# An attention-and-MLP kernel: VectorE's share of the exponentials in five instructions instead of eight, with eight tile buffers and a new order of the work

## The chip, the cores and the metric

The kernel runs on one core of a Trainium2 chip. The metric is the device time of one execution in microseconds (us); the time given for a kernel is the median of its runs.

## The reference

The input x has 2048 rows of 448 numbers. Two layers follow one another, and each layer is an attention block A and a mixing block B, each on the normalised x and each added to x:

```python
x = x + _A_ref(_layernorm(x), A_wqkv, A_wo)
x = x + _B_ref(_layernorm(x), B_w1, B_w2, B_w3, B_w4)
...
scores = jnp.einsum("bhqd,bhkd->bhqk", q, k) * (Dh ** -0.5)   # 16 heads, Dh = 28
p = _softmax(scores, axis=-1)
o = jnp.einsum("bhqk,bhkd->bhqd", p, v)
...
h  = _gelu(_layernorm(x) @ w1)                  # 448 -> 448
hs = shifted_quarters(h) @ w2                   # columns moved by -1, +1, -2, +2 rows
x1 = x + hs
return x1 + _gelu(_layernorm(x1) @ w3) @ w4     # 448 -> 1792 -> 448
```

The softmax needs 2 layers x 16 heads x 2048 x 2048 exponentials.

## The kernel before

**Tiles.** The rows are 16 tiles of 128. Attention works on score blocks of 128 keys by 512 entries (512 queries of one head, or, in the last two chunks of a layer, 256 queries of one head for two key tiles). Four heads form a group g. A segment is one chunk of queries, one group and a range of key tiles; there are 68 segments, 2048 blocks in all, and they are worked off in a fixed order (`segs`, `stream`). The number of a pair of segments is the key of the tables `R_RATE` and `D_RATE`; the number of four segments is the key of `XPAR["dt", ...]` and its like.

**The way of a block.** TensorE makes the scores in PSUM (`score_ops`, L1487). ScalarE takes two or three neighbouring PSUM banks in one instruction, applies the exponential and writes bf16 tiles to the ring `PT` (`t_exp`, L1754). TensorE multiplies the tiles with the values (`t_pv`, L831) into PSUM bank 7, four heads side by side, and the last row gives the sum for the softmax's division (`t_norm`). There is no search for a maximum: a bound from the norms of q and k stands as a further row of the matrices, so each score arrives in PSUM shifted.

**Blocks for VectorE.** Some blocks go to VectorE instead of ScalarE. `d_first` (L1584) reads the scores from PSUM, multiplies them by log2(e) times 256 and stores int16 in a buffer `y`; `d_chain` (L1611 to L1624) shapes this integer in seven instructions into the bits of the bf16 exponential and writes it to a slot of `PD`: cut out the fraction (L1611), a straight line of it (L1613), its square (L1615), a straight line of the square (L1617), product (L1619), add to the integer (L1621), undo the offset and shift (L1624). There are two `y` buffers, four `PD` slots and three `fb` buffers; in two stretches of the run (`t_extra`) free parts of `vaug` give two more `y`, one more `fb` and one more `PD`. A `y` is held from before `d_first` to the end of the chain, a `PD` slot until TensorE has multiplied the block.

**Which blocks.** `t_scores` builds units of three and two blocks by turns, three PSUM banks for each. On a unit of three it may replace the third by a block from 6 to 8 steps ahead for VectorE (the ring way, `R_RATE`), if VectorE was busy in the last 3 us by less than `XPAR["dt", ...]`. It may add to any unit a block from 5 to 7 steps ahead in one of the two spare banks (the spare way, `D_RATE`), if the filler matmuls took at least the share `XPAR["ft", ...]` of the last 8 us. The two tables limit how many blocks of a segment may go each way, and each block needs a free `y` and a free `PD` slot at that moment.

**Order.** Nothing is decided on the chip. When the kernel is built, `Sched` runs the generators as tasks over modelled durations (`DST` holds those of the chain's instructions), and the order that comes out is each engine's fixed instruction list, with semaphore waits between engines. Tasks have a rank (`RANK`, smaller first); a chain's rank is `XPAR["dp", ...]` (up to 3.2) and becomes 1.0 when its block is about to be multiplied. Where TensorE would idle, `keep_pe_busy` puts in filler matmuls on `ident` (L2267), whose results nobody reads. Evictions from PSUM (L2196, L2005, L1226, L1838 and others), normalisation and additions to x run on VectorE between the chains. For a few operations `XPAR["ex", ...]` and similar entries say whether GpSimd (0), VectorE (1) or whichever is earlier (2) takes them. `PE_NORM` says for the last group of a chunk whether the softmax's division is spread with DMAs on the SP queue or with small matmuls.

## Time and profile before

| | |
|---|---|
| median of three runs | 1026.12 us (1024.83 to 1026.28) |
| profiled execution, span from first to last instruction | 1023.9 us |
| ScalarE busy / TensorE busy / VectorE busy / GpSimd busy | 973.6 / 973.4 / 843.5 / 220.1 us |
| blocks on ScalarE: units of three / of two | 332 / 459 |
| blocks on VectorE | 134 |
| granted TensorE clock | 1.000 |

The profile of the execution has a span; the time of a run is longer by what lies around it. Engines are PE (TensorE, with its weight loads as PEld), DVE (VectorE), ACT (ScalarE), POOL (GpSimd) and SP (the DMA queue). A row of the groups view gives line, engine, operation, output<-input with shapes, count, busy time and mean duration, and the engine's idle time just before with what ended it. A row of the windows view gives a stretch of the span, its length, and each engine's busy time and number of instructions in it. Because 332 x 3 + 459 x 2 = 1914 blocks pass ScalarE and 134 pass VectorE, all 2048 are accounted for.

### The profile page before, as it was taken

The page shows a single profiled execution, that of the slowest core. Times are in us where ns is not written, and L with a number is a line of the kernel's source. Part 1 is how long each engine was busy: PE and PEld are TensorE (multiplying, and loading weights), DVE is VectorE, ACT ScalarE, POOL GpSimd, SP SyncE. Part 2 cuts the span into 40 slices and gives each one's busy share as a digit, 9 for nine tenths or more (in the row PEclk, how much of TensorE's full clock was granted, in tenths as well). Part 3 has the DMA queues.
Part 4 walks back from the last instruction along what each step waited for, and adds up shares of the span by engine and source line. Part 5 has one row for each costly group of instructions (what it writes and reads, how often), then busy time and mean ns, then how long its engine had stood idle before and what let it go on. Part 6 is the DMA issues. An engine that isn't in the chain of part 4 may idle for free.

```text
span 1023.9 us, 36349 instructions
## 1 busy us (share of the span) xinstructions
PE 973.4 (95%) x16102; PEld 404.7 (40%) x16102; DVE 843.5 (82%) x2134; ACT 973.6 (95%) x897; POOL 220.1 (21%) x350
## 2 busy tenths in 40 slices
PE   8999899999999999999999999999999999999998
PEld 4333344334343334344344333333333333444465
DVE  8879999988768778897788888997898888788752
ACT  6899999999999999999999999999999999999942
POOL 4003022143213013350212010112332200331220
PEclk9999999999999999999999999999999999999999
DMA  4534228121203113321133024324311110220000
GB/s 126 130 74 140 59 76 216 34 44 37 33 18 84 43 49 88 51 39 19 36 87 63 22 76 140 112 80 112 74 29 33 32 55 13 55 61 17 13 21 25
DMA packets 98829, 64.43 MB, mean 63 GB/s; under 512 B 70832, under 2 KB 87552, under 8 KB 98672
## 3 DMA queue, kind: packets, MB, share of 16 engines
q1 hardware_dynamic: 94176, 53.11, 21.1%
q0 software_dynamic: 3376, 8.09, 3.0%
q8 instruction: 126, 2.06, 0.9%
q10 hardware_dynamic: 1120, 0.92, 0.3%
q14 instruction: 31, 0.25, 0.1%
HBM read 28.16 MB, written 16.76 MB: 44 GB/s over the span
## 4 chain that ended last, share of the span: by engine, by line
ACT 62%; PE 23%; DVE 12%; DMA 1%; issue 1%; ACTq 0%; SPq 0%; DVEq 0%
ACT PT L1754 55%; PE ps L840 12%; PE ps L1487 5%; PE ps L831 4%; ACT h2T L2220 3%; PE ps L2267 1%; ACT fb L2036 1%; DVE yd L1584 1%; DMA xT<-xnd 1%; DVE fb L1619 1%; DVE fb L1615 1%; DVE PD L1624 1%; DVE ub L1840 1%; DVE vaug L1621 1%; ACT L1754 1%
## 5 line engine op out<-in xcount | busy, mean ns | idle before, releaser
L1754 ACT ACTIVATE PT<-ps 128x1024 bf16<-128x1024 f32 (+1 forms) x791 | 877.8, 1288 | 7.8 <-PE ps L1487 6.6
L1487 PE MATMUL ps<-qT,kT 32*128 32x512 bf16 (+1 forms) x2560 | 310.1, 340 | 23.5 <-ACT PT L1754 17.7
L831 PE MATMUL ps<-PT,vaug 128*32 128x512 bf16 (+1 forms) x2396 | 243.8, 341 | 0.5 <-ACT PT L1754 0.3
L1487 PEld LDWEIGHTS ps<-qT,kT 32*128 32x128 bf16 x2560 | 79.7, 91 | 292.0 <-ACT PT L1754 262.9
L840 PE MATMUL ps<-xT,w 128*32 128x512 bf16 (+3 forms) x2592 | 178.7, 343 | 1.7 <-issue 0.8
L2267 PE MATMUL ps<-ident 128*32 128x256 bf16 x2508 | 123.0, 280 | 2.2 <-POOL ident L930 1.5
L831 PEld LDWEIGHTS ps<-PT,vaug 128*32 128x32 bf16 x2396 | 71.8, 94 | 91.5 <-issue 78.2
L840 PE MATMUL ps<-w,h2T 128*32 128x448 bf16 x1288 | 89.5, 355 | 2.0 <-ACT h2T L2220 2.0
L840 PEld LDWEIGHTS ps<-xT,w 128*32 128x32 bf16 (+1 forms) x2592 | 68.9, 95 | 52.5 <-issue 25.1
L2267 PEld LDWEIGHTS ps<-ident 128*32 128x32 bf16 x2508 | 73.1, 98 | 25.3 <-issue 9.2
L1584 DVE TENSOR_SCALAR yd<-ps 128x512 int16<-128x512 f32 x94 | 64.5, 686 | 21.8 <-PE ps L1487 21.1
L1865 POOL TENSOR_TENSOR otn<-ub,fb 128x512 bf16<-128x512 f32 (+1 forms) x32 | 37.2, 1162 | 189.3 <-DMA fb<-rscr 178.7
L2196 DVE CAST h2T<-ps 128x384 bf16<-128x384 f32 (+1 forms) x84 | 52.0, 619 | 19.7 <-PE ps L840 17.9
L1615 DVE TENSOR_TENSOR fb<-fb 128x512 bf16<-128x512 int16 x112 | 49.0, 438 | 0.7
L840 PEld LDWEIGHTS ps<-w,h2T 128*32 128x32 bf16 x1288 | 34.6, 96 | 31.0 <-issue 12.0
L831 PE MATMUL ps<-PD,vaug 128*32 128x512 bf16 (+1 forms) x146 | 43.9, 342 | 1.2 <-DVE PD L1624 1.0
L840 PE MATMUL ps<-xT,wk_pad 128*32 128x512 bf16 (+1 forms) x512 | 41.2, 369 | 1.8 <-DVE kT L1226 1.2
L2267 PE MATMUL ps<-ident,xn 128*32 128x256 bf16 x896 | 40.8, 274 | 0.6 <-DVE ub L1840 0.6
L840 PE MATMUL ps<-wo_pad,otn 128*32 128x448 bf16 x512 | 36.9, 355 | 3.2 <-DVE x_res L1920 1.7
L1621 DVE TENSOR_TENSOR yd<-yd,fb 128x512 int16<-128x512 int16 x88 | 38.3, 436 | 1.2
L840 PE MATMUL ps<-wv,xT 128*32 128x448 bf16 x480 | 37.7, 356 | 0.6 <-ACT kT L1227 0.2
L840 PE MATMUL ps<-xT,wq_pad 128*32 128x512 bf16 x448 | 36.8, 382 | 1.4 <-DVE kT L1226 0.8
(238 smaller groups left out, 1318.0 us busy)
## 6 DMA issues: line engine op xcount, KB each, us to landing
uscr<-ub SPq DMA_DIRECT2D x28, 256.0 KB
ub<-uscr SPq DMA_DIRECT2D x28, 256.0 KB
fb<-rscr SPq DMA_DIRECT2D x96, 64.0 KB, 2.1
xnd<-xn SPq DMA_DIRECT2D x28, 128.0 KB, 3.1
x_res<-in_A_x_dram POOLq DMA_DIRECT2D x16, 224.0 KB, 3.3
xd<-x_res SPq DMA_DIRECT2D x16, 224.0 KB, 2.3
x_res<-xd SPq DMA_DIRECT2D x16, 224.0 KB, 4.1
out_dram<-obf SPq DMA_DIRECT2D x16, 112.0 KB, 1.8
```

Source lines behind the costliest of these rows:

```text
L831: return lambda e: e.matmul(out=out, lhsT=lhsT, rhs=rhs, start=start, stop=stop, **kw)
L840: r.append(e.matmul(out=out[c:c + w, :], lhsT=lhsT[:, c:c + w], rhs=rhs, start=start, stop=stop, tile_position=(0, c)))
L1487: yield op("pe", (0.005 + NW * 0.00042) / nc_, lambda e, i=i, kc=kc, j=j, g=g, a=a, NW=NW, bank=bank: e.matmul(out=ps[:, bank, i * NW:(i + ...
L1584: yield op("dve", c_ps(512), lambda e: e.tensor_scalar(out=y.bitcast(I16)[:, 0:512], in0=ps[:, bi(bank), :], scalar1=SCALE * L2E * FS, sca ...
L1615: yield op("dve", D_[2], lambda e: e.tensor_tensor(out=z, in0=qa, in1=qa, op=ALU.mult), reads=fk, writes=fk, urge=urge, two=True)
L1619: yield op("dve", D_[4], lambda e: e.tensor_tensor(out=z, in0=z, in1=w, op=ALU.mult), reads=yk + fk, writes=fk, urge=urge, two=True)
L1621: yield op("dve", D_[5], lambda e: e.tensor_tensor(out=ya, in0=ya, in1=z, op=ALU.add), reads=yk + fk, writes=yk, urge=urge, two=True)
L1754: yield op("act", 0.0635 + n * w * 0.000833, lambda e, bk=bk, s0=s0, n=n, w=w: e.activation(out=PT[:, s0:s0 + n, 0:w], in_=ps[:, bk[0]:bk[ ...
L1865: yield both(("eo", L, ch), 0.2 + NW * 0.0021, 0.07 + NW * 0.00104, lambda e: e.tensor_tensor(out=otn[:, g, 0:NW], in0=u, in1=rb[:, 0:NW], ...
L2196: ev = op("dve", c_ps(m * NW), lambda e, hr=hr, pv=pv: e.tensor_copy(out=hr, in_=pv), reads=[("ps", bi(b))], writes=hk, touch=[b])
L2220: yield op("act", c_act(len(fr_) * NW), lambda e, v=v: e.activation(out=v, in_=v, func=ACT.Gelu_apprx_tanh), reads=allk, writes=allk, tab= ...
L2267: return [e.matmul(out=ps[32 * c:32 * c + 32, bi(b), 0:256].rearrange("p (a n) -> p a n", n=128), lhsT=xn[:, 0, D:D + 32] if live else ide ...
```

## The change

- The bound added to the scores grows by 127 ln 2 (`WSH`), so that the scaled score already contains the exponent offset of a bf16 number; ScalarE's exponential takes it away again in its bias (`XB`).
- `d_first` scales by 128 instead of 256 and writes int16 straight into the block's `PD` slot (or slot of `vaug`). The chain has four instructions instead of seven: mask the seven fraction bits, a straight line of the fraction, times the fraction, add to the integer in place. `yd` is gone, and `fb` still holds the two temporaries.
- `NPD` is 8 instead of 4; the extra stretches give one `fb` and five slots instead of two `y`, one `fb` and one slot. A block needs one free slot and no `y`.
- A task may set its rank later (`"prio"`); tasks that had their `RANK` from the start now get it behind their first waits.
- New values stand in `R_RATE`, `D_RATE`, `Q_LEAD`, `RANK`, `PE_NORM` and `XPAR`. Summed over the segments, with `4 x steps x rate` rounded up for each way and at most two blocks for a step, both tables together allow 670 blocks for VectorE before and 670 after; the ring way alone 276 before and 348 after, the spare way alone 498 and 434. The threshold `dt` of the ring way rises in 15 of its 17 entries, and six are above 1 afterwards. The entries that fix VectorE for an operation go from 10 to 14 (`ex`), 4 to 5 (`ez`), 2 to 1 (`eo`) and 5 to 7 (`ek`). `PE_NORM` turns to matmuls for chunks 0 and 2 of the second layer. `XPAR["l0"]` goes from 10 to 9.

```diff
--- before.py
+++ after.py
@@ -262,6 +262,8 @@
...
+            elif c == "prio":
+                t[0] = spec[1]
...
@@ -547,9 +549,9 @@
...
-DST = [0.2, 0.2, 0.336, 0.2, 0.336, 0.336, 0.2]
+DST = [0.2, 0.2, 0.336, 0.336]
...
-R_RATE = {(0,): 0, (1,): 0.006, (2,): 0.016, (3,): 0.04, (4,): 0.006, (5,): 0.051, (6,): 0.059, (7,): 0, (8,): 0.06, (9,): 0.048, (10,): 0.024, (11,): 0.15, (12,): 0.066, (13,): 0.022, (14,): 0.022, (15,): 0.192, (16,): 0.233, (17,): 0.075, (18,): 0.115, (19,): 0.273, (20,): 0.093, (21,): 0.233, (22,): 0.355, (23,): 0.29, (24,): 0, (25,): 0.268, (26,): 0.146, (27,): 0.207, (28,): 0.183, (29,): 0.243, (30,): 0.071, (31,): 0.163, (32,): 0.241, (33,): 0.078}
+R_RATE = {(0,): 0, (1,): 0.017, (2,): 0, (3,): 0.289, (4,): 0, (5,): 0, (6,): 0.464, (7,): 0.077, (8,): 0.08, (9,): 0.083, (10,): 0.142, (11,): 0.145, (12,): 0.099, (13,): 0.203, (14,): 0.073, (15,): 0.235, (16,): 0.205, (17,): 0, (18,): 0, (19,): 0.124, (20,): 0.16, (21,): 0.455, (22,): 0.25, (23,): 0.495, (24,): 0.01, (25,): 0.114, (26,): 0.241, (27,): 0.325, (28,): 0.097, (29,): 0.329, (30,): 0.157, (31,): 0.364, (32,): 0.014, (33,): 0.064}
...
@@ -559,10 +561,10 @@
...
-D_RATE = {(0,): 0, (1,): 0.177, (2,): 0, (3,): 0.517, (4,): 0.133, (5,): 0.289, (6,): 0.447, (7,): 0.362, (8,): 0.067, (9,): 0.088, (10,): 0.129, (11,): 0.262, (12,): 0, (13,): 0.687, (14,): 0.003, (15,): 0.526, (16,): 0, (17,): 0.061, (18,): 0.049, (19,): 0.1, (20,): 0.403, (21,): 0.327, (22,): 0.258, (23,): 0, (24,): 0.164, (25,): 0.165, (26,): 0.245, (27,): 0, (28,): 0.523, (29,): 0.61, (30,): 0.121, (31,): 0.077, (32,): 0.657, (33,): 0.301}
...
+D_RATE = {(0,): 0.037, (1,): 0, (2,): 0.58, (3,): 0.194, (4,): 0.479, (5,): 0.586, (6,): 0.437, (7,): 0.328, (8,): 0.51, (9,): 0.193, (10,): 0.104, (11,): 0, (12,): 0, (13,): 0.576, (14,): 0.047, (15,): 0.097, (16,): 0.523, (17,): 0.148, (18,): 0, (19,): 0.123, (20,): 0, (21,): 0.203, (22,): 0.271, (23,): 0.126, (24,): 0.168, (25,): 0.205, (26,): 0.053, (27,): 0.008, (28,): 0, (29,): 0.135, (30,): 0.368, (31,): 0.683, (32,): 0, (33,): 0.709}
...
@@ -572,7 +574,7 @@
...
@@ -608,7 +610,7 @@
...
-    WSH = 60.0 / SCALE
+    WSH = (60.0 + 127.0 * math.log(2.0)) / SCALE
...
@@ -617,11 +619,12 @@
...
-    FS = 256.0
+    FS = 128.0
+    XB = math.log(0.99835146) - 127.0 * math.log(2.0)
...
-    EA, EB, EG = 21.0427, 88.0467, -0.244205
+    EG, EB = 0.33575143 / 128.0, -0.34288473
...
-    NPD = 4
+    NPD = 8
...
     def c_ps(n):
@@ -740,7 +743,6 @@
...
-        yd = sb("yd", [128, 2, 512], I32)
...
@@ -1537,7 +1543,7 @@
         def xtra(kind):
...
-                    return {"y": ["yv%d" % base, "yv%d" % (base + 2)], "f": ["fv%d" % (base + 4)], "pd": ["pv%d" % (base + 6)]}[kind]
+                    return {"f": ["fv%d" % base], "pd": ["pv%d" % (base + k) for k in range(2, 7)]}[kind]
...
         def t_extra(ph, base):
...
@@ -1561,12 +1567,6 @@
...
-        def ybuf(r):
-            if r[1] == "v":
-                v, k = vbuf(r)
-                return v.bitcast(I32), k
-            return yd[:, num1(r), :], [("yd", num1(r))]
-
         def fbuf(r):
...
@@ -1577,53 +1577,46 @@
...
-        YS = ["y0", "y1"]
-
-        def d_first(blk, bank, ys, pd, ring=None):
-            y, yk = ybuf(ys)
-            yield op("dve", c_ps(512), lambda e: e.tensor_scalar(out=y.bitcast(I16)[:, 0:512], in0=ps[:, bi(bank), :], scalar1=SCALE * L2E * FS, scalar2=-126.0 * FS, op0=ALU.mult, op1=ALU.max),
-                     reads=[("ps", bi(bank))], writes=yk, touch=[bank])
+
+        def ibuf(blk):
+            key, s = home[blk]
+            return (vaug if key == "vaug" else PD)[:, s, :], (key, s)
+
+        def d_first(blk, bank, pd, ring=None):
+            y, yk = ibuf(blk)
+            yield op("dve", c_ps(512), lambda e: e.tensor_scalar(out=y.bitcast(I16), in0=ps[:, bi(bank), :], scalar1=SCALE * L2E * FS, scalar2=0.0, op0=ALU.mult, op1=ALU.max),
+                     reads=[("ps", bi(bank))], writes=[yk], touch=[bank])
...
                 yield ("rel", bank)
...
                 yield ("dead", bank)
                 yield ("sig", ("dx", ring))
-            yield ("spawn", d_chain(blk, ys, pd), XPAR["dp", blk[0] // 4])
+            yield ("spawn", d_chain(blk), XPAR["dp", blk[0] // 4])
...
-        def d_chain(blk, ys, pd):
+        def d_chain(blk):
...
-            y, yk = ybuf(ys)
-            ya, yu, w = y.bitcast(I16)[:, 0:512], y.bitcast(U16)[:, 0:512], y.bitcast(BF16)[:, 512:1024]
-            key, s = home[blk]
-            pk = (key, s)
-            pdt = (vaug if key == "vaug" else PD)[:, s, :]
+            y, yk = ibuf(blk)
+            ya, yu = y.bitcast(I16), y.bitcast(U16)
...
             def urge():
...
-            fr = yield ("acq", xtra("f") + FB, yk)
+            fr = yield ("acq", xtra("f") + FB, [yk])
...
-            qu, qa, z = q.bitcast(U16)[:, 0:512], q.bitcast(I16)[:, 0:512], q.bitcast(BF16)[:, 512:1024]
+            fu, w = q.bitcast(U16)[:, 0:512], q.bitcast(BF16)[:, 512:1024]
...
-            yield op("dve", D_[0], lambda e: e.tensor_scalar(out=qu, in0=yu, scalar1=8, scalar2=32768, op0=ALU.logical_shift_left, op1=ALU.bitwise_xor),
-                     reads=yk, writes=fk, urge=urge, two=True)
-            yield op("dve", D_[1], lambda e: e.tensor_scalar(out=w, in0=qa, scalar1=EA / 65536.0, scalar2=EB, op0=ALU.mult, op1=ALU.add),
-                     reads=fk, writes=yk, urge=urge, two=True)
-            yield op("dve", D_[2], lambda e: e.tensor_tensor(out=z, in0=qa, in1=qa, op=ALU.mult),
+            yield op("dve", D_[0], lambda e: e.tensor_scalar(out=fu, in0=yu, scalar1=127, scalar2=None, op0=ALU.bitwise_and),
+                     reads=[yk], writes=fk, urge=urge, two=True)
+            yield op("dve", D_[1], lambda e: e.tensor_scalar(out=w, in0=fu, scalar1=EG, scalar2=EB, op0=ALU.mult, op1=ALU.add),
...
-            yield op("dve", D_[3], lambda e: e.tensor_scalar(out=z, in0=z, scalar1=1.0 / 65536.0 ** 2, scalar2=EG, op0=ALU.mult, op1=ALU.add),
+            yield op("dve", D_[2], lambda e: e.tensor_tensor(out=w, in0=w, in1=fu, op=ALU.mult),
...
-            yield op("dve", D_[4], lambda e: e.tensor_tensor(out=z, in0=z, in1=w, op=ALU.mult),
-                     reads=yk + fk, writes=fk, urge=urge, two=True)
-            yield op("dve", D_[5], lambda e: e.tensor_tensor(out=ya, in0=ya, in1=z, op=ALU.add),
-                     reads=yk + fk, writes=yk, urge=urge, two=True)
+            yield op("dve", D_[3], lambda e: e.tensor_tensor(out=ya, in0=ya, in1=w, op=ALU.add),
+                     reads=[yk] + fk, writes=[yk], urge=urge, two=True)
             yield ("rel", fr)
-            yield op("dve", D_[6], lambda e: e.tensor_scalar(out=pdt.bitcast(U16), in0=yu, scalar1=32768, scalar2=1, op0=ALU.bitwise_xor, op1=ALU.logical_shift_right),
-                     reads=yk, writes=[pk], urge=urge, two=True)
-            yield ("rel", ys)
             yield from finished(blk)
...
         def t_scores():
@@ -1688,9 +1681,9 @@
                         rb = ahead_of(un[-1][0], un[-1][1], R_RATE, RLO, RHI, [b_[2] for b_ in un])
                         got = None
                         if rb is not None:
-                            got = yield ("try", [xtra("y") + YS, xtra("pd") + PDS])
+                            got = yield ("try", [xtra("pd") + PDS])
                         if got is not None:
-                            take(rb, R_RATE, got[1])
+                            take(rb, R_RATE, got[0])
...
                         rb = 0
@@ -1719,19 +1712,19 @@
...
-                    extra.append((rb, ("b2", got[0], got[1], u)))
+                    extra.append((rb, ("b2", got[0], u)))
...
-                        got = yield ("try", [MISC[0:2], xtra("y") + YS, xtra("pd") + PDS])
+                        got = yield ("try", [MISC[0:2], xtra("pd") + PDS])
                         if got is not None:
-                            take(blk, D_RATE, got[2])
+                            take(blk, D_RATE, got[1])
...
                 yield from score_ops(blks, banks)
                 for blk, got in extra:
-                    yield ("spawn", d_first(blk, *got), 1 if len(got) == 3 else XPAR["rp", si0 // 4])
+                    yield ("spawn", d_first(blk, *got), 1 if len(got) == 2 else XPAR["rp", si0 // 4])
                 yield ("sig", ("st", u))
...
@@ -1751,7 +1744,7 @@
...
-                yield op("act", 0.0635 + n * w * 0.000833, lambda e, bk=bk, s0=s0, n=n, w=w: e.activation(out=PT[:, s0:s0 + n, 0:w], in_=ps[:, bk[0]:bk[0] + n, 0:w], func=ACT.Exp, scale=SCALE, bias=math.log(2.0)),
+                yield op("act", 0.0635 + n * w * 0.000833, lambda e, bk=bk, s0=s0, n=n, w=w: e.activation(out=PT[:, s0:s0 + n, 0:w], in_=ps[:, bk[0]:bk[0] + n, 0:w], func=ACT.Exp, scale=SCALE, bias=XB),
...
                     yield ("dead", "b%d" % b)
@@ -1904,6 +1897,7 @@
         def t_outproj(L, ch):
...
             yield ("wait", ("segstart", seg_of[(L, ch, 0)][-1]))
+            yield ("prio", RANK["o", L, ch])
...
                 yield ("spawn", t_xload(L, t0 + tt), 4)
             yield ("wait", ("loaded", "wo"))
...
```

26 lines of the change are left out of this document (15 added, 11 removed).

## The prediction

> **What bounds the kernel now.** I read the page first: which engine is full, and what the chain that ended last is made of.
>
> ```profile
> span 1023.9 us, 36349 instructions
> PE 973.4 (95%) x16102; PEld 404.7 (40%) x16102; DVE 843.5 (82%) x2134; ACT 973.6 (95%) x897; POOL 220.1 (21%) x350
> ACT 62%; PE 23%; DVE 12%; DMA 1%; issue 1%; ACTq 0%; SPq 0%; DVEq 0%
> ```
>
> ScalarE and TensorE are both at 95%, and ScalarE holds 62% of the chain. An average hides where, so next come the windows of all engines, with the cuts at the first steady exponentials, at 256, 640 and 832, and at the last exponential. Below it stand the windows of the chain's first instruction (L1584) and those of the filler matmuls (L2267), over the same stretches.
>
> ```profile
> 22.00:256.00 234.00, 219.31 (x3414) 87.41 (x3418) 209.77 (x559) 225.46 (x206) 51.50 (x69) 1.00 0.35 89
> 256.00:640.00 384.00, 371.23 (x6073) 146.58 (x6065) 307.94 (x734) 383.11 (x344) 78.53 (x138) 1.00 0.24 57
> 640.00:832.00 192.00, 181.41 (x2787) 71.21 (x2784) 172.85 (x454) 191.26 (x172) 45.37 (x60) 1.00 0.27 67
> 832.00:971.00 139.00, 133.36 (x2364) 57.97 (x2360) 114.88 (x285) 138.92 (x129) 29.30 (x49) 1.00 0.14 33
> 971.00:1024.00 53.00, 49.19 (x1161) 31.48 (x1154) 19.67 (x41) 19.55 (x29) 6.35 (x15) 1.00 0.08 25
> ...
> 22.00:256.00 234.00, 27.36 (x40) 1.00 0.35 89
> 256.00:640.00 384.00, 27.43 (x40) 1.00 0.24 57
> 640.00:832.00 192.00, 25.02 (x37) 1.00 0.27 67
> 832.00:971.00 139.00, 12.04 (x18) 1.00 0.14 33
> ...
> 22.00:256.00 234.00, 68.52 (x1448) 40.71 (x1448) 1.00 0.35 89
> 256.00:640.00 384.00, 24.42 (x592) 16.34 (x592) 1.00 0.24 57
> 640.00:832.00 192.00, 46.94 (x956) 26.85 (x956) 1.00 0.27 67
> 832.00:971.00 139.00, 10.82 (x224) 6.74 (x224) 1.00 0.14 33
> ```
>
> In a row the busy times stand in the order PE, PEld, DVE, ACT, POOL. From 22 to 971 us ScalarE works 938.75 of 949 us: this stretch lasts as long as ScalarE's work. TensorE looks nearly as full, but part of that is filler. What is neither idle nor filler leaves TensorE 83 us of slack in the first stretch (234 - 219.31 + 68.52), 37 in the second, 57 in the third and 16 in the fourth. So ScalarE sets the time to 971, and behind it comes a tail of 53 us that no exponential enters, with TensorE busy for 49. VectorE, over the first four rows, is busy for 805.4 us, 84.9% of the stretch; its fullest rows (90%) are the first and third, where 40 and 37 of its 134 blocks lie. The block counts add to 135, since one block stands on a cut.
>
> **The chain of a block.** The groups view gives each instruction of the chain, in the form that occurs most.
>
> ```profile
> L1584 DVE TENSOR_SCALAR yd<-ps 128x512 int16<-128x512 f32 x94 | 64.5, 686 | 21.8 <-PE ps L1487 21.1
> L1615 DVE TENSOR_TENSOR fb<-fb 128x512 bf16<-128x512 int16 x112 | 49.0, 438 | 0.7
> L1621 DVE TENSOR_TENSOR yd<-yd,fb 128x512 int16<-128x512 int16 x88 | 38.3, 436 | 1.2
> L1619 DVE TENSOR_TENSOR fb<-fb,yd 128x512 bf16<-128x512 bf16 x88 | 37.6, 428 | 0.6
> L1617 DVE TENSOR_SCALAR fb<-fb 128x512 bf16<-128x512 bf16 x112 | 34.4, 308 | 0.8
> L1613 DVE TENSOR_SCALAR yd<-fb 128x512 bf16<-128x512 int16 x88 | 26.6, 306 | 0.9
> L1611 DVE TENSOR_SCALAR fb<-yd 128x512 uint16<-128x512 uint16 x88 | 26.3, 303 | 0.4
> L1624 DVE TENSOR_SCALAR PD<-yd 128x512 uint16<-128x512 uint16 x86 | 26.3, 306 | 1.4
> ```
>
> Before: 0.686 + 0.303 + 0.306 + 0.438 + 0.308 + 0.428 + 0.436 + 0.306 = 3.211 us. The new chain keeps L1584's form (f32 from PSUM to int16, 0.686), one 16-bit masking like L1611 (0.303), one straight line like L1613 (0.306), one product of 16-bit tiles like L1619 (0.428) and the addition of L1621 (0.436): 2.159 us. Gone are a square, a straight line and the last shift, 1.052 us. The mixed product (bf16 by uint16) occurs nowhere; its neighbours L1615 and L1619 take 0.438 and 0.428 with either kind of operand, so it is bounded by these, and in-place writing by the in-place addition L1621. The 134 blocks thus free 141 us of VectorE. By itself this gains nothing, since VectorE isn't the bound; the gain comes only from blocks that it takes from ScalarE.
>
> Busy durations count the overlap of neighbours twice, as this stretch of the time order shows:
>
> ```profile
> 330.01 0.29 DVE L1617 TENSOR_SCALAR fb<-fb 128x512 bf16<-128x512 bf16 x1
> 330.22 0.29 DVE L1624 TENSOR_SCALAR PD<-yd 128x512 uint16<-128x512 uint16 x1
> 330.42 0.69 DVE L2196 CAST h2T<-ps 128x512 bf16<-128x512 f32 x1
> ```
>
> A step of 0.29 us lets the next one start after 0.20 us when the two are independent. [...]
>
> **What a block is worth on ScalarE.**
>
> ```profile
> L1754 ACT ACTIVATE PT<-ps 128x1024 bf16<-128x1024 f32 (+1 forms) x791 | 877.8, 1288 | 7.8 <-PE ps L1487 6.6
> ...
> L1754 ACT ACTIVATE PT<-ps 128x1536 bf16<-128x1536 f32 x332 | 503.2, 1540 | 5.9 <-PE ps L1487 5.3
> L1754 ACT ACTIVATE PT<-ps 128x1024 bf16<-128x1024 f32 x459 | 482.3, 1106 | 1.8 <-PE ps L1487 1.3
> ```
>
> 332 x 3 + 459 x 2 = 1914 blocks in 877.8 us are 0.459 us each. A block of the ring way only shortens a unit from three to two: 1.540 - 1.106 = 0.434 us. I take 0.45, between the two.
>
> **How many blocks move.** That is the unknown, and the traces don't hold it. The limits of the tables are no guide: 134 of 670 allowed were taken, and 670 are allowed again. What limited the choice was VectorE's load, the two `y` buffers outside the extra stretches, and the fillers' share. The change relaxes the first two. So I bound the number by VectorE's share of the stretch. Other work on VectorE in it is 805.4 - 134 x 3.211 = 375 us. The fixed choices add some 8 us to that (four more additions to x, one more square for the gelu, eight squares for the k bound and two divisions by matmul with its small copies, with 0.62, 0.68, 0.39 and about 1 us each from their rows, less one multiplication handed back):
>
> ```profile
> L2120 DVE TENSOR_TENSOR x_res<-x_res,x1b 128x448 f32<-128x448 f32 x11 | 6.8, 621 | 0.1
> L2034 DVE TENSOR_TENSOR fb<-vaug 128x512 f32<-128x512 bf16 x7 | 4.7, 684 | 0.0
> L1257 DVE TENSOR_TENSOR obf<-kT 128x512 bf16<-128x512 bf16 (+2 forms) x12 | 4.7, 392 | 0.3
> ```
>
> With N blocks the stretch is 949 - 0.45 (N - 134), and VectorE's share s of it is 383 + 2.159 N. At s = 0.80, the share of the second row, N is 168 and 15.5 us are gained. At today's 0.849 N is 186 and the gain 23.6 us. At 0.92, a little over today's fullest row, N is 212 and the gain 35.1 us. I take s = 0.86: eight slots instead of two `y` let the second and fourth rows (80 and 83%) come nearer to the other two, but a part of VectorE's gaps there is waiting for scores, 21.1 us in L1584's row, which no buffer mends. N is then 190.5, 56 blocks move, and the stretch gets 25.4 us shorter.
>
> **What else is on the path.** Spread by length, that gain asks 6, 10, 5 and 4 us of the four stretches, less than TensorE's slack of 83, 37, 57 and 16 us; the fillers go first. The clock is granted in full (1.00 in every row), and the fillers left hold it. The tail is left as it is: its blocks and matrices are the same, and only new ranks touch it. For the new order I can't derive a size; I bound it by -4 and +6 us, some tenth of the tail each way, and take 0. The two divisions that turn to matmuls take 12 small DMAs off the SP queue and a multiplication each off GpSimd, which is busy for 21%. On TensorE they add ten small matmuls each, about 3 us, covered by fillers in the stretches with slack. One wait moves: the first instruction of a chain now writes a slot that TensorE has read, which the last one (L1624) did before, and VectorE's evictions stand behind it. L1624's row shows 1.4 us of idle time for 86 of them, so for 190 the cost lies between nothing and 3 us; eight slots give the product more time to be over, so I take nothing. The rank set later, the new bias of the exponential and the larger bound add no instruction. The bigger scores are scaled by the same instructions.
>
> **The sum.** The span goes from 1023.9 to 998.5 us. The median of the runs, 1026.12, lies 2.2 us above the profiled span, so the time predicted is 1000.7 us, a gain of 2.5%. A change within 0.2%, 2 us, can't be told from none here.
>
> **The rivals.**
> *TensorE bounds the middle and the end.* For it: with the fillers left in, TensorE is busy for 371 of 384 us and 133 of 139. Then only the blocks of the first and third stretches pay: 77 x 1.052 = 81 us freed, over 2.159 + 0.9 x 0.45 = 2.56 us for a block gives 32 blocks and 14.2 us, 1011.9 us. Against it: the slack without fillers, 37 and 16 us. [...]
>
> *The number doesn't rise.* The limits of both tables together are the same, and the spare way still asks for fillers, of which few are left from 256 to 640 us. Then ScalarE's work stays and the time is 1024 to 1028 us. Against it: 15 of 17 thresholds of the ring way rise, and the `y` buffers are gone.
>
> *Slower: blocks come late for the product.* TensorE takes its list in order. If a chain isn't ready when its block is to be multiplied, the next scores wait behind it, and ScalarE with them. Now this is rare:
>
> ```profile
> PEld ps L831 <- DVE PD L1624: 2.7, 5, 1.4
> L831 PE MATMUL ps<-PD,vaug 128*32 128x512 bf16 (+1 forms) x146 | 43.9, 342 | 1.2 <-DVE PD L1624 1.0
> ```
>
> Some 6 of 134 blocks are late, by 0.54 us in the mean of the five. With chains at low rank on a fuller VectorE, lateness eats the gain of 25.4 us once 47 of 190 blocks are late by that much. With 90 late, 48.6 us are lost, and the time is 1024 us plus 25.
>
> **How the numbers follow.** The forecast (a gain by 50 to 80 further blocks or fewer, 991 to 1010) gets 0.63; TensorE as the bound (1007 to 1016) 0.17; a larger gain, with VectorE over 92% or a shorter tail (below 988) 0.06; an unchanged number 0.05; late blocks 0.09. Faster by over 0.2% are the first three, 0.86; of the fourth nearly all lies within 0.2%, 0.04, and the rest, with the late blocks, is slower, 0.10. The range reaches from s = 0.92 with the better end of the order (about 987) to the far side of the TensorE rival, 1015; a little under 2 in 10 stays outside.
>
> **What would show it.** Right: chains of five instructions of 0.69, 0.30, 0.31, 0.43 and 0.44 us; some 190 of the first; some 1858 blocks on ScalarE and L1754 near 852 us; the last exponential near 945; a tail of about 53 us; fillers fewer by about 25 us. TensorE as the bound would show in ScalarE idle before L1754, waiting for L1487, in the second and fourth stretches, or in a longer tail. Late blocks would show as TensorE waiting for the chain's last addition. The prediction fails above all if N does: each block is worth 0.45 us.

## The result, and the profile after

The changed kernel's median is 1013.42 us (1012.83 to 1014.19), against 1026.2 us of the kernel before on the same chip: a ratio of 0.9876, interval 0.9862 to 0.989. It is faster, by 12.8 us. That is half of the 25.4 us forecast, and 1.5 us from the 1011.9 us of the rival in which TensorE bounds the middle and the end. The profiled span went from 1023.9 to 1010.8 us, 13.1 us less.

The page of the changed kernel, its head and the line that gives the chain by engine:

```profile
span 1010.8 us, 35186 instructions
PE 965.7 (96%) x15538; PEld 392.6 (39%) x15538; DVE 857.5 (85%) x2109; ACT 944.5 (93%) x908; POOL 213.3 (21%) x343
...
ACT 62%; PE 31%; DVE 5%; issue 1%; ACTq 0%; POOL 0%; DVEq 0%
```

TensorE's part of the chain has grown from 23 to 31%, and ScalarE's busy share has fallen from 95 to 93%. ScalarE, which was to set the time, now has holes. Next, the groups of the exponentials and of VectorE's chain in the changed kernel (line, engine, operation, output<-input, count, busy time, mean ns, idle time before):

```profile
L1747 ACT ACTIVATE PT<-ps 128x1024 bf16<-128x1024 f32 (+1 forms) x798 | 848.2, 1230 | 10.5 <-PE ps L1493 9.7
...
L1587 DVE TENSOR_SCALAR PD<-ps 128x512 int16<-128x512 f32 x166 | 113.5, 686 | 16.7 <-PE ps L1493 14.5
L1615 DVE TENSOR_TENSOR fb<-fb 128x512 bf16<-128x512 bf16 x179 | 80.0, 450 | 1.4
L1617 DVE TENSOR_TENSOR PD<-PD,fb 128x512 int16<-128x512 int16 x149 | 61.6, 416 | 1.2
L1613 DVE TENSOR_SCALAR fb<-fb 128x512 bf16<-128x512 uint16 x179 | 52.9, 301 | 1.2
L1611 DVE TENSOR_SCALAR fb<-PD 128x512 uint16<-128x512 uint16 x149 | 42.0, 291 | 0.3
L1587 DVE TENSOR_SCALAR vaug<-ps 128x512 int16<-128x512 f32 x42 | 28.6, 684 | 4.2 <-PE ps L1493 3.7
```

The chain takes 0.686 + 0.291 + 0.301 + 0.450 + 0.416 = 2.144 us (forecast 2.159). VectorE has 166 + 42 = 208 blocks: 74 more than before, not 56. ScalarE's exponentials went from 877.8 to 848.2 us, 29.6 us less, which is more than the 25.4 that was asked of them. Yet only 13.1 us came out. The windows of all engines in the changed kernel (PE, PEld, DVE, ACT, POOL, then the granted clock), cut as before but at its own last exponential, show where the rest stayed:

```profile
22.00:256.00 234.00, 222.97 (x3316) 84.77 (x3316) 203.89 (x527) 226.25 (x217) 50.64 (x65) 1.00 0.34 89
256.00:640.00 384.00, 371.32 (x6029) 145.66 (x6027) 336.74 (x798) 374.15 (x349) 80.37 (x139) 1.00 0.24 60
640.00:832.00 192.00, 181.29 (x2561) 66.35 (x2557) 171.70 (x416) 184.85 (x173) 37.24 (x55) 0.99 0.26 62
832.00:958.00 126.00, 122.04 (x2157) 54.75 (x2153) 108.23 (x267) 124.89 (x121) 28.49 (x49) 0.99 0.13 29
```

ScalarE works 910.1 of the 936 us up to 958 and idles 25.9; before, it idled 10.3 of 949. The new idle time lies in the second row (384 - 374.15 = 9.9 against 0.9 before) and the third (7.2 against 0.7). The tail is what it was: the last exponential ends at 956.35, 54.5 us ahead of the end, before at 970.47 and 53.4. ScalarE's waits in the changed kernel (engine and line, what ended the wait, us, times, longest) name the places:

```profile
ACT PT L1747 <- PE ps L1493: 9.7, 14, 2.8
ACT h2T L2214 <- DVE h2T L2190: 6.2, 1, 6.2
ACT fct L1438 <- DVE dbc L1452: 4.3, 1, 4.3
```

And the time order on ScalarE around them (start, duration, and in brackets the idle time before and what ended it):

```profile
471.77 1.06 ACT L2012 ACTIVATE hT<-hT 112x1024 bf16<-112x1024 bf16 x1 [2.35 <-DVE hT L1999]
479.04 6.18 ACT L2214 ACTIVATE h2T<-h2T 128x7168 bf16<-128x7168 bf16 x1 [6.21 <-DVE h2T L2190]
...
652.08 0.20 ACT L1438 ACTIVATE fct<-dbc 128x4 f32<-128x4 f32 x1 [4.28 <-DVE dbc L1452]
653.17 3.28 ACT L1747 ACTIVATE PT<-ps 128x1536 bf16<-128x1536 f32 x3 [0.89 <-PE ps L1493]
```

The two holes hold 2.35 + 6.21 + 4.28 + 0.89 = 13.7 us; before, ScalarE's row of 256 to 640 had 0.9 us of idle time in all. The first lies at the layer boundary. The last exponential of the first layer ends at 468 us, and those of the second start at 486; between them ScalarE waits for the mixing block of tiles 7 to 10 (L2190), and the second layer's first queries stand behind that block on TensorE. How early the first layer had been is seen where VectorE takes a finished segment from PSUM (L1838 before, L1831 after). These are the segments 30 and 32, the last but one of the first layer and the first of the second, in the time order of the kernel before:

```profile
474.04 0.42 DVE L1838 COPY ub<-ps 128x256 f32<-128x256 f32 x1 [0.18 <-PE ps L831]
...
509.37 0.68 DVE L1838 COPY ub<-ps 128x512 f32<-128x512 f32 x1
```

and of the changed kernel:

```profile
455.75 0.41 DVE L1831 COPY ub<-ps 128x256 f32<-128x256 f32 x1
...
500.82 0.68 DVE L1831 COPY ub<-ps 128x512 f32<-128x512 f32 x1
```

A lead of 18.3 us at segment 30 is 8.6 us at segment 32: 9.7 us are lost across the boundary, about the 8.56 us of ScalarE's waits there. (The lead also swings where nothing is lost, since other work stands in other places: it is 22.7 us at segment 23, 13.3 at 25 and 20.2 at 29.) The attention of the first layer went ahead, but what the second layer's first queries need did not. The fourth addition to x that closes the mixing block of a tile moved from 366.74 to 389.23 us, and the bound from the second layer's first keys (L1420 before, L1426 after) from 422.86 to 461.95.

The place of the queries changed too. In TensorE's time order of the kernel before, they start at 431 us, and the mixing block (`xT,w`) later takes turns with scores (L1487), so that ScalarE is fed:

```profile
430.97 0.61 PE L840 MATMUL ps<-xT,wq_pad 128*32 128x512 bf16 x8 [0.48 <-DMA xT<-xnd]
...
487.34 0.70 PE L840 MATMUL ps<-xT,w 128*32 128x512 bf16 x8
487.97 0.39 PE L1487 MATMUL ps<-qT,kT 32*128 32x512 bf16 x2
```

In the changed kernel the end of the block and the queries are one piece without scores:

```profile
471.46 6.73 PE L842 MATMUL ps<-xT,w 128*32 128x512 bf16 x112 [0.36 <-DVE h2T L2190]
478.17 3.85 PE L842 MATMUL ps<-xT,wq_pad 128*32 128x512 bf16 x64
```

TensorE also had less room. Its fillers (L2267) and its busy time from 320 to 480 us, before:

```profile
320.00:480.00 160.00, 13.22 (x316) 9.03 (x316) 1.00 0.26 56
...
320.00:480.00 160.00, 153.61 (x2691) 62.16 (x2695) 131.11 (x321) 159.58 (x144) 39.92 (x64) 1.00 0.26 56
```

and after (L2261):

```profile
320.00:480.00 160.00, 4.74 (x96) 2.83 (x96) 1.00 0.25 58
...
320.00:480.00 160.00, 154.93 (x2679) 60.33 (x2670) 136.14 (x324) 151.30 (x142) 39.71 (x69) 1.00 0.25 58
```

Of 160 us TensorE had 19.6 free before by these rows (13.2 of filler and 6.4 idle), and 9.8 after. That is too much: a filler's row overlaps its neighbours. By the start and the modelled end of every matmul in the trace, all that isn't filler leaves 15.2 us before and 7.5 after. ScalarE's idle time in this window grew by 8.3 us (8.7 after 0.4).

### The profile page after: what moved, and what is told of

Read it like the earlier page. It is cut to its first block, busy times and chain, and to the rows that moved or that the text cites. A ratio compares the mean times of both kernels' runs of the same rounds, so it can differ in the third digit from the quotient of the medians.

```text
span 1010.8 us, 35186 instructions
## 1 busy us (share of the span) xinstructions
PE 965.7 (96%) x15538; PEld 392.6 (39%) x15538; DVE 857.5 (85%) x2109; ACT 944.5 (93%) x908; POOL 213.3 (21%) x343
## 4 chain that ended last, share of the span: by engine, by line
ACT 62%; PE 31%; DVE 5%; issue 1%; ACTq 0%; POOL 0%; DVEq 0%
ACT PT L1747 56%; PE ps L842 17%; PE ps L1493 8%; PE ps L833 6%; ACT h2T L2214 3%; ACT fb L2030 1%; PE ps L2261 1%; DVE PD L1587 1%; ACT L1747 1%; ACT hT L2012 1%; DVE vaug L1336 0%; DVE ub L1833 0%; DVE fb L1615 0%; ACT L2012 0%; DVE x_res L1914 0%
## 5 line engine op out<-in xcount | busy, mean ns | idle before, releaser
L1747 ACT ACTIVATE PT<-ps 128x1024 bf16<-128x1024 f32 (+1 forms) x798 | 848.2, 1230 | 10.5 <-PE ps L1493 9.7
L842 PE MATMUL ps<-xT,w 128*32 128x384 bf16 (+4 forms) x2592 | 163.9, 335 | 1.2 <-DVE h2T L2190 1.1
L1587 DVE TENSOR_SCALAR PD<-ps 128x512 int16<-128x512 f32 x166 | 113.5, 686 | 16.7 <-PE ps L1493 14.5
L842 PE MATMUL ps<-w,h2T 128*32 128x448 bf16 x1288 | 89.3, 355 | 2.6 <-ACT h2T L2214 2.4
L2261 PE MATMUL ps<-ident 128*32 128x256 bf16 x1884 | 86.7, 280 | 1.6 <-POOL ident L932 1.5
L842 PEld LDWEIGHTS ps<-xT,w 128*32 128x32 bf16 (+1 forms) x2592 | 67.1, 95 | 51.2 <-issue 20.9
L1615 DVE TENSOR_TENSOR fb<-fb 128x512 bf16<-128x512 bf16 x179 | 80.0, 450 | 1.4
L2190 DVE CAST h2T<-ps 128x384 bf16<-128x384 f32 (+1 forms) x84 | 52.1, 620 | 13.3 <-PE ps L842 12.6
L1617 DVE TENSOR_TENSOR PD<-PD,fb 128x512 int16<-128x512 int16 x149 | 61.6, 416 | 1.2
L833 PE MATMUL ps<-PD,vaug 128*32 128x512 bf16 (+1 forms) x216 | 61.9, 337 | 0.0
L2261 PEld LDWEIGHTS ps<-ident 128*32 128x32 bf16 x1884 | 52.4, 98 | 20.2 <-issue 6.1
L1613 DVE TENSOR_SCALAR fb<-fb 128x512 bf16<-128x512 uint16 x179 | 52.9, 301 | 1.2
L842 PEld LDWEIGHTS ps<-w,h2T 128*32 128x32 bf16 x1288 | 33.1, 96 | 32.0 <-issue 16.3
L2261 PE MATMUL ps<-ident,xn 128*32 128x256 bf16 x916 | 44.3, 274 | 0.3 <-DVE ub L1833 0.3
L842 PE MATMUL ps<-wo_pad,otn 128*32 128x448 bf16 x512 | 40.1, 360 | 2.6 <-DVE x_res L1914 2.6
L1611 DVE TENSOR_SCALAR fb<-PD 128x512 uint16<-128x512 uint16 x149 | 42.0, 291 | 0.3
```

Source lines behind the costliest of these rows:

```text
L833: return lambda e: e.matmul(out=out, lhsT=lhsT, rhs=rhs, start=start, stop=stop, **kw)
L842: r.append(e.matmul(out=out[c:c + w, :], lhsT=lhsT[:, c:c + w], rhs=rhs, start=start, stop=stop, tile_position=(0, c)))
L1587: yield op("dve", c_ps(512), lambda e: e.tensor_scalar(out=y.bitcast(I16), in0=ps[:, bi(bank), :], scalar1=SCALE * L2E * FS, scalar2=0.0, ...
L1611: yield op("dve", D_[0], lambda e: e.tensor_scalar(out=fu, in0=yu, scalar1=127, scalar2=None, op0=ALU.bitwise_and), reads=[yk], writes=fk, ...
L1613: yield op("dve", D_[1], lambda e: e.tensor_scalar(out=w, in0=fu, scalar1=EG, scalar2=EB, op0=ALU.mult, op1=ALU.add), reads=fk, writes=fk, ...
L1615: yield op("dve", D_[2], lambda e: e.tensor_tensor(out=w, in0=w, in1=fu, op=ALU.mult), reads=fk, writes=fk, urge=urge, two=True)
```

## The experiments

All experiments start from the changed kernel unless the text says otherwise, and where durations alone are cut the order of the instructions stays as it is. "The changed kernel" below is 1013.42 us, ratio 0.9876.

**The two halves of the change.** First the chain alone, with the six tables of the kernel before (`R_RATE`, `RANK`, `Q_LEAD`, `D_RATE`, `PE_NORM`, `XPAR`), so that the planner makes another order for the new chain.

```diff
-R_RATE = {(0,): 0, (1,): 0.017, ...      # and the other five tables of the changed kernel
+R_RATE = {(0,): 0, (1,): 0.006, ...      # those of the kernel before
```

> The five-instruction chain, the eight slots and the shifted scores, with all six tables of the kernel before. If the chain by itself brings the gain (141 us of VectorE freed, and the buffers gone as a limit): 1000 to 1015 us with some 180 blocks on VectorE. If the tables' shares and thresholds set the number of blocks: 130 to 155 blocks and 1020 to 1030 us.

Measured: 1033.46 us, ratio 1.0074 (1.0059 to 1.0089), slower than before. Then the kernel before with the new tables:

```diff
-R_RATE = {(0,): 0, (1,): 0.006, ...
+R_RATE = {(0,): 0, (1,): 0.017, ...
```

> The kernel before, with its eight instructions, two y buffers and four slots, but with the six tables of the changed kernel. If the new order is good by itself: 1015 to 1026 us. If it was made for the short chain: 1040 to 1065 us, since VectorE then has 3.2 us for each of as many blocks or takes fewer.

Measured: 1060.85 us, ratio 1.034 (1.0324 to 1.0355). The old chain takes 146 blocks with them, 12 more. So neither half gains anything by itself; each loses, by 7 and 35 us, and together they win 13. With the old tables the new chain does move blocks (135 into `PD` and 37 into `vaug`, 172 in all, 38 more than 134), as its groups view shows for `PD`, and then ScalarE waits for scores, by its waits view:

```profile
L1587 DVE TENSOR_SCALAR PD<-ps 128x512 int16<-128x512 f32 x135 | 92.1, 687 | 28.2 <-PE ps L1493 26.3
...
ACT PT L1747 <- PE ps L1493: 28.1, 15, 12.4
```

28.1 us in 15 waits, one of 12.4: 38 blocks are worth 15 to 17 us on ScalarE, and one order gives more than that back. The order is not a small term beside the blocks; here it decides the sign.

**Which engine is full.** Four runs cut one engine each. ScalarE's exponentials of the first layer (from unit 20 on) write 448 of 512 columns, so the other 64 keep old values:

```diff
+                wx = 448 if 20 <= u and un[-1][0] < 32 else w
-                ... e.activation(out=PT[:, s0:s0 + n, 0:w], in_=ps[:, bk[0]:bk[0] + n, 0:w], func=ACT.Exp, ...
+                ... e.activation(out=PT[:, s0:s0 + n, 0:wx], in_=ps[:, bk[0]:bk[0] + n, 0:wx], func=ACT.Exp, ...
```

> The changed kernel with its order kept, but ScalarE's exponentials of the first layer (from the 21st unit on) work on 448 of 512 columns; the rest of each tile keeps old numbers, so this kernel leaves out an eighth of that softmax work. That takes about 64 columns x 0.85 ns = 0.054 us from each of some 870 blocks, 47 us of ScalarE. Theory A (up to about 650 us the end is set by the first layer's way through TensorE to the last keys of the second layer, and ScalarE only waits there): 1007 to 1014 us, and the wait at about 650 us grows from 4 us to some 40. Theory B (ScalarE sets the time everywhere and the two holes are accidents): 965 to 980 us. Theory C (VectorE's evictions come late): near A, 1005 to 1014.

Measured: 1005.02 us, ratio 0.9802 (0.9787 to 0.9816): 8.4 us less. ScalarE's busy time fell by 30.6 us, from 944.5 to 913.9, not by the 47 estimated. The same cut in the second layer (`un[0][0] >= 32`):

> The same cut, but in the second layer's exponentials only (448 of 512 columns, an eighth of that work left out). Theory A: only what lies behind the wait at 650 us pays, some 570 blocks of 0.054 us, 31 us: 980 to 990 us, or 990 to 1003 where TensorE then bounds the end. Theory B: all 900 blocks pay, 45 us and more: 963 to 972 us.

Measured: 1005.37 us, ratio 0.9805 (0.9788 to 0.9821): 8.0 us less, with ScalarE busy for 910.8 us, outside what I expected. ScalarE's waits in the first of the two say where the rest went:

```profile
ACT PT L1748 <- PE ps L1493: 27.7, 75, 2.8
...
ACT h2T L2215 <- DVE h2T L2191: 6.2, 1, 6.2
ACT fct L1438 <- DVE dbc L1452: 4.3, 1, 4.3
```

Waiting for scores grows from 9.7 to 27.7 us, in 75 waits of 2.8 us at most, and the two long waits keep their 6.2 and 4.3 us, though ScalarE is there earlier. So a faster ScalarE meets TensorE at once, and the unchanged holes fit a fixed list in which the same TensorE work stands behind the scores. Then TensorE: two of four contraction steps of the first layer's wide projection run on 64 of 512 columns, so that product is incomplete.

```diff
+                        NX = 64 if L == 0 and fc in (1, 2) else NW
-                        ... ps[:, bi(b), k * NW:(k + 1) * NW], w3[...], xv(xt)[:, fc, 0:NW], ...
+                        ... ps[:, bi(b), k * NW:k * NW + NX], w3[...], xv(xt)[:, fc, 0:NX], ...
```

> The changed kernel with its order kept, but two of the four contraction steps of the first layer's wide projection (448 to 1792) work on 64 of 512 columns: about 0.187 us x 2 x 14 x 4 = 21 us of TensorE left out before 600 us. Theory A with TensorE's throughput as the cause: the two holes of 8.6 and 5.2 us mostly close, 999 to 1006 us. Theory B: 1012 to 1014 us. Theory C: 1010 to 1014 us.

Measured: 1010.07 us, ratio 0.9849 (0.9833 to 0.9865): 3.3 us less, although the projections (L842) from 256 to 640 us took 210.85 instead of 229.30 us. And VectorE: the last four instructions of each chain of the first layer on 128 columns, so three quarters of those blocks stay unfinished.

```diff
+            if si < 32:
+                ya, yu = ya[:, 0:128], yu[:, 0:128]
...
+            if si < 32:
+                fu, w = fu[:, 0:128], w[:, 0:128]
```

> The changed kernel with its order kept, but the last four instructions of each chain of the first layer work on 128 of 512 columns: about 0.6 us x 103 blocks = 60 us of VectorE left out. Theory A with TensorE's throughput: 1009 to 1014 us. Theory C (VectorE's evictions are late and hold the first layer up): 998 to 1006 us, with the holes closed. Theory B: 1012 to 1014 us.

Measured: 1012.31 us, ratio 0.9874 (0.985 to 0.9898): no gain clear of the interval, though VectorE's busy time fell from 857.5 to 800.1 us. VectorE is not the bound, at 85% or at 79%. None of the three theories stands: A had asked for a wait of some 40 us at 650 us in the first cut (it is 4.3) and for 1006 us or less in TensorE's, B for 980 us or less in the first, C for 1006 or less in VectorE's.

**Two engines together.** The first ScalarE cut and the TensorE cut in one kernel:

> Both cuts in the first layer together, order kept: the exponentials on 448 of 512 columns (an eighth of that work left out) and two of four contraction steps of the wide projection on 64 of 512 columns. Each alone gave 8.4 and 3.3 us against the changed kernel. Theory D (TensorE and ScalarE are both full in the first layer, so that time falls only where both get shorter): clearly more than the sum, 18 us or more, 985 to 996 us. Theory E (latencies of the chain from tile to tile, through DMAs, hold the first layer): the sum or less, 1001 to 1006 us.

Measured: 997.42 us, ratio 0.9721 (0.9695 to 0.9748): 16.0 us less, where the cuts alone gave 8.4 and 3.3. That is more than their sum, 11.7, and less than the 18 us that theory D asked for. The four runs reach from 994.42 us (granted clock 1.000) to 999.85 (0.993), so the 4.3 us above the sum are loose in size, but all four lie below the 1001.7 us of the sum. Part of what each cut frees comes through only when the other engine is cut as well. The same pair in the second layer:

```diff
+                wx = 448 if un[0][0] >= 32 else w
...
+                        NX = 64 if L == 1 and fc in (1, 2) else NW
```

> Exponentials of the second layer on 448 of 512 columns (as in the run with ScalarE's second-layer cut, 8.0 us faster than the changed kernel) and two of the four contraction steps of the second layer's wide projection on 64 columns (as in the first-layer TensorE cut, 3.3 us alone). If both engines are full together in the second layer as in the first, where the two cuts gave 16.0 us for 8.4 and 3.3 alone, the last exponential ends 12 to 18 us earlier than in the changed kernel (956.4), at 938 to 944; if ScalarE waits for something else there, it ends near 948 to 950 as with its cut alone. The tail after it gets shorter too, by 3 to 8 us, since the last blocks of the wide projection lie in it and TensorE is busy 50 of its 53 us; that part is no evidence.

Measured: 992.87 us, ratio 0.9692 (0.9661 to 0.9724). The part that is evidence is the last exponential. In the time order of ScalarE in the changed kernel, in the kernel with ScalarE's second-layer cut alone, and in this one (the last row of exponentials in each; the last run of them ends at start plus duration, 956.3, 947.8 and 940.9):

```profile
952.86 3.47 ACT L1747 ACTIVATE PT<-ps 128x1024 bf16<-128x1024 f32 x3
```

```profile
943.50 4.30 ACT L1748 ACTIVATE PT<-ps 128x1344 bf16<-128x1344 f32 x4 [0.26 <-PE ps L1493]
```

```profile
936.82 4.11 ACT L1748 ACTIVATE PT<-ps 128x1344 bf16<-128x1344 f32 x4 [0.19 <-PE ps L1493]
```

15.4 us earlier with both cuts, 8.5 with ScalarE's alone, within the 12 to 18 expected of two full engines. TensorE's cut alone wasn't run in the second layer, so it isn't shown there that the pair gives more than the sum. In both layers ScalarE alone does not set the time; that the two engines set it together is shown for the first and likely for the second.

**The boundary.** If ScalarE's wait at 468 to 479 is what ate the lead, taking work out of exactly that block should give it back, and the same cut one block earlier should not. All four steps of the wide projection of tiles 7 to 10 on 64 columns, and the evictions too, so most of that product is missing:

```diff
+                        NX = 64 if L == 0 and tiles[0] == 7 else NW
...
+                    if L == 0 and tiles[0] == 7:
+                        hr, pv = hr[:, 0:64], pv[:, 0:64]
```

> The wide-projection block of tiles 7 to 10 of the first layer (line 2169 of the changed kernel) is cut to 64 of 512 columns, its 14 evictions (line 2190) too; the order of all instructions is the changed kernel's. That takes about 11.8 us from TensorE (224 matmuls of 0.060 us each, by the row of 112 in 6.73 us, times 7/8) and about 7 us from VectorE. This block is the one behind which ScalarE idled 2.35 and 6.21 us at 468 to 479. If the gain went to waits at the layer boundary, the two idle stretches go and most of the cut with them: 7 to 10 us faster than the changed kernel, 1003 to 1006 us. If TensorE's work is worth the same everywhere, 3.3 us per 18.5 us as in the run with TensorE's first-layer cut, it is 2 us: 1011.

and the control, the same with `tiles[0] == 3`:

> The same cut of the same number of instructions, in the block before it (tiles 3 to 6 of the first layer, evictions from 349 to 376), where ScalarE does not wait; the order is the changed kernel's. If place decides: within 2 us of the changed kernel, 1011 to 1013. If TensorE's work is worth the same everywhere, it is equal to the other cut.

Measured: 1015.11 us, ratio 0.9904 (0.9877 to 0.9931), and 1015.6 us, ratio 0.9898 (0.9884 to 0.9913). Both theories missed: neither cut gains. ScalarE's time order in the first of them shows the block's waits shrink, from 8.56 to 1.72 + 1.34 = 3.06 us, and two new ones appear behind them:

```profile
472.99 1.06 ACT L2012 ACTIVATE hT<-hT 112x1024 bf16<-112x1024 bf16 x1 [1.72 <-DVE hT L1999]
475.39 6.18 ACT L2217 ACTIVATE h2T<-h2T 128x7168 bf16<-128x7168 bf16 x1 [1.34 <-DVE h2T L2193]
...
486.59 1.94 ACT L1747 ACTIVATE PT<-ps 128x1024 bf16<-128x1024 f32 x2 [3.72 <-PE ps L1493]
490.67 9.45 ACT L1747 ACTIVATE PT<-ps 128x1024 bf16<-128x1024 f32 x10 [2.15 <-PE ps L1493]
```

Gained 5.5 us, lost 3.72 + 2.15 = 5.9. TensorE's time order, and its windows of ten microseconds (busy time, granted clock), say why:

```profile
478.63 1.90 PE L842 MATMUL ps<-xT,wq_pad 128*32 128x512 bf16 x16 [3.63 <-DMA xT<-xnd]
...
460.00:470.00 10.00, 8.81 (x170) 0.66 0.18 41
470.00:480.00 10.00, 4.69 (x198) 0.84 0.29 56
480.00:490.00 10.00, 9.23 (x133) 0.82 0.01 2
```

With the block gone, the next late thing is the load of the second layer's first queries (`xT` from `xnd`), and 3.63 us of waiting for it. Then 16 matmuls of the projection take 1.90 us; in the changed kernel, 32 of them take 1.94. The clock had been taken away: it is 1.00 in each of these three windows of the changed kernel. In the control it fell further:

```profile
345.00:350.00 5.00, 4.89 (x65) 0.50 0.52 130
```

So these two runs do not measure what the work of a block is worth; they measure a cut together with the clock that it costs. What the first does show is that the boundary is two things in series, the block and the queries behind it. That the boundary ate the lead is thus not proven by them. The clean versions weren't tried: the block gone with the clock held, or only the queries moved ahead of the block, where the kernel before has them.

**The fillers.** The pair of first-layer cuts again, and the filler matmuls on 32 of their 256 columns:

```diff
-            return [e.matmul(out=ps[..., 0:256]..., rhs=ident[:, :].unsqueeze(1).to_broadcast([128, 2, 128]), ...
+            return [e.matmul(out=ps[..., 0:32], ..., rhs=ident[:, 0:32], ...
```

> As the run before, and each filler matmul on 32 of 256 columns (fillers compute nothing that is read). Theory D, with fillers that stand in TensorE's fixed list and hold up the scores behind them: 5 to 20 us less than without. If fillers only fill idle time: within 2 us of the run before, or longer if the granted clock falls.

Measured: 1013.34 us, ratio 0.9869 (0.983 to 0.9908), against 997.42 with full fillers: lighter fillers cost 16 us. Whether fillers also hold up scores can't be read from it, because the clock fell. In the third stretch, the windows of the kernel with the pair and of this one (PE, PEld, DVE, ACT, POOL, clock):

```profile
640.00:832.00 192.00, 183.24 (x2538) 66.15 (x2535) 172.50 (x418) 188.97 (x177) 37.36 (x55) 0.98 0.24 54
```

```profile
640.00:832.00 192.00, 178.20 (x2440) 59.59 (x2442) 168.01 (x403) 183.40 (x170) 36.69 (x55) 0.89 0.23 54
```

The clock falls from 0.98 to 0.89 there, and over the whole run to 0.969, 0.956, 0.953 and 0.959 in the four executions.

**A version with a smaller second hole.** Nine entries of the tables are changed and nothing is left out; the last keys of the second layer and their bound come earlier on TensorE.

```diff
 RANK:   ("b", 1, 0) 2.813 -> 3      ("a", 1, 1) 2.429 -> 2.371   ("k", 1, 4) 1.325 -> 1
         ("c", 1, 4) 1.146 -> 1      ("w", 0, 4) 1.161 -> 1
 Q_LEAD: (1, 0) 109 -> 113           D_RATE: (31,) 0.683 -> 0.693
 XPAR:   ("ek", 1, 4) 2 -> 1         ("wt", 10) 0.38 -> 0.457
```

> The changed kernel with nine entries of its tables changed (four ranks of the second layer's mixing and keys and one of the first layer's, the start of the first queries of the second layer, one rate, two entries of XPAR), so that the last keys of the second layer and their bound come earlier. Nothing is left out. If the waits at fixed places are what the gain was lost to, ScalarE's wait before line 1438 (4.28 us at 648 to 652) falls to about 2 us, a smaller wait may appear ahead of it, and the kernel is 1 to 3 us faster than the changed kernel: 1010.5 to 1012.5. If TensorE has no room there, the wait is only moved and the time is 1013 to 1014.

Measured: 1007.28 us (1006.92 to 1007.99), ratio 0.9819 (0.9806 to 0.9833). It beats both kernels, the changed one by 6.1 us, and by more than either theory gave. ScalarE's time order in it:

```profile
617.81 7.87 ACT L1747 ACTIVATE PT<-ps 128x1024 bf16<-128x1024 f32 x8 [1.18 <-PE ps L833]
...
650.50 0.20 ACT L1438 ACTIVATE fct<-dbc 128x4 f32<-128x4 f32 x1 [1.03 <-DVE dbc L1452]
```

The wait before L1438 is 1.03 us instead of 4.28, for one new wait of 1.18 ahead of it. In the ends of the segments, as VectorE takes them from PSUM, this version is 2.2 us behind the changed kernel at segment 46 and 1.8 ahead at 47: the smaller hole is worth 3.9 us, and the delay ahead of it takes 2.2 of them. But it gains again where no hole was, 2.2 us between segments 51 and 53 (688 to 706 us) and 1.4 between 64 and 65 (914 to 930). There the clock differs. TensorE's windows (busy time, granted clock) in the changed kernel:

```profile
690.00:700.00 10.00, 8.83 (x80) 0.91 0.50 101
700.00:710.00 10.00, 10.00 (x129) 0.92 0.19 62
...
920.00:930.00 10.00, 10.00 (x152) 0.83 0.16 28
```

and in this version:

```profile
690.00:700.00 10.00, 9.60 (x110) 1.00 0.51 134
```

It has 1.00 from 700 to 710 and from 920 to 930 too. So 3.6 of the 6.1 us come with a clock that didn't dip, and all five runs of this version have a mean of 0.998 or 1.000, where the four of the changed kernel have 0.995 to 0.997. ScalarE waited 0.56 + 0.81 + 0.27 us for scores around 700 us in the changed kernel, and not at all in this one. That the order is the reason for the dip is likely but not shown, since the moment at which a dip comes may differ for other reasons.

## Why the prediction was wrong

*The chain, 3.211 to 2.159 us: right,* 2.144 measured. The mixed product, bounded by 0.428 and 0.438, takes 0.450 us in `fb` and, by the groups view, 0.416 in `vaug`:

```profile
L1615 DVE TENSOR_TENSOR vaug<-vaug 128x512 bf16<-128x512 bf16 x29 | 12.1, 416 | 0.3
```

*The number of blocks: too low,* 74 more instead of 56. VectorE's share came out at 0.877 over the four rows (820.6 of 936 us), near the 0.86 taken, and the blocks fit because the stretch stayed longer than forecast and VectorE's other work is 820.6 - 208 x 2.144 = 374.6 us, not 383; the 8 us that were added for the fixed choices don't show.

*The value of a block: a little high,* 29.6 us for 74 blocks, 0.40 us each instead of 0.45. ScalarE's units of three went from 332 to 244 and those of two from 459 to 554, so the mean price of what stays rose from 0.459 to 848.2/1840 = 0.461. The two errors pull in opposite directions, by luck: 29.6 us of ScalarE saved against 25.4.

*"ScalarE sets the time to 971" and "TensorE's slack covers the gain": this is the step that failed.* The stretch got 14.1 us shorter for 29.6 us of work, and ScalarE's idle time grew by 15.6, of which 13.7 stand in the two holes. The cuts show the step itself to be wrong: 30.6 us less of ScalarE in the first layer yield 8.4 us, TensorE's cut alone 3.3, both 16.0. The working compared a gain of 10 us in the second stretch with 37 us of slack, and had three faults. The slack was counted too high, since filler rows overlap their neighbours: by the start and end of every matmul it was 54, 30, 37 and 12 us in the four stretches, not 83, 37, 57 and 16. It lay elsewhere: from 320 to 480 us there were 15.2. And the second stretch was not cut at the boundary between the layers, which asks for a whole chain (mixing block, keys and their bound, queries) before ScalarE can go on; that chain came later, the bound by 39 us and the queries by 47, while the attention came 18 us earlier. How much of the loss is TensorE's lack of room and how much is the place where the new order puts the block and the queries stays open: no run moves the queries alone, and the two runs on the block lost their clock.

*The new order, taken as nothing: wrong as a bound.* -4 to +6 us was a tenth of the tail; the runs of the two halves give +7 and +35 us against the kernel before, and nine table entries -6 against the changed one. Neither the chain nor the tables gain without the other. The 13.7 us at 468 and 652 us are half of the forecast gain, and another order took the second hole down to 1.03 + 0.89 us, for 1.18 us ahead of it.

*"The fillers left hold the clock": not quite.* It dipped to 0.91 and 0.83 in the two places shown, which cost up to 3.6 us by the comparison with the last version; before it was 1.00 in every stretch.

*The rivals.* TensorE as the bound of the middle came nearest, 1011.9 against 1013.42 us, and its sign was there: ScalarE's waits for scores before L1747 rise from 6.6 to 9.7 us. That its number is so near is luck, since it counted on 32 further blocks and 74 moved. And the larger part of the idle time stands in front of other instructions (L2012, L2214, L1438), and the end of the run is not where it lies: the fourth stretch has 126 - 124.89 = 1.1 us of it. What speaks for this rival in the runs: with TensorE's matmuls busy for 96% of the changed kernel's span and its weight loads for 39%, ScalarE's cuts yield a quarter of their size (8.4 of 30.6 us, 8.0 of 33.7) and the first layer's pair more than its sum (16.0 us against 11.7). Late blocks didn't come: of TensorE's waits for the chain's last addition (L1617) the waits view holds 0.5 us on the weight loads, so eight slots and the moved wait cost nothing, as taken. The number that doesn't rise was far off.

*The tail: right,* 54.5 us for about 53. *The fillers: right,* 122.7 us instead of 150.7 over the four stretches, 28 fewer for a forecast of about 25.

## What to carry to other kernels

Where two engines are both near 95%, as here, work taken from one may be worth only what the other lets through; price it by cutting both in one run, and cut each in its own run beside it. Slack is counted without the overlap of filler rows and up to the next point at which everything must be there (a layer boundary, a first query), not over a long stretch, and the questions are what must be done by then and where the fixed order puts it. A part of a change that only makes another order can decide the sign (here +7 and +35 us for the halves, and 6 us more gain by nine entries of a table), so it is bounded by what an order of this kernel can cost, not by a share of its tail.

## What the hardware did that I had not expected

In the control run TensorE lost half its clock without any long pause. The first narrow matmuls (64 columns, L842) come at 338.7 us, the longest pause of TensorE from there to 345 us is 0.36 us, and the clock goes to 0.79 from 340 to 345 and to 0.50 from 345 to 365, with TensorE busy for 19.8 of those 20 us. The changed kernel's own two dips come too with no pause of TensorE over 1 us after the first 30 us (the longest is 0.96 us, at 318.7). With narrow fillers the clock fell too (0.89 over 192 us). Whether it is the narrow matmuls that take the clock away, and how, these runs don't tell. With the pair of first-layer cuts, fillers of 256 columns nearly held it (a mean of 0.993 to 1.000 in four runs) and fillers of 32 did not (0.953 to 0.969); widths between weren't run. So in this kernel TensorE time that a change sets free should be filled as wide as here, and a cut of TensorE's work in an experiment has to be read beside its clock.
